# Where the identity matrix comes from: GpSimd's iota replaced by a VectorE construction in a normalised-attention kernel

## The chip, the cores and the metric

The kernel runs on one core of one Trainium2 chip. A core has five engines that work side by side and meet only at semaphores: TensorE (PE, matrix products, with its weight loads listed apart as PEld), VectorE (DVE), ScalarE (ACT, activation functions), GpSimd (POOL) and SyncE (SP, which here only starts DMAs). The metric is the device time of one execution in microseconds (us), as the median of several runs; less is better.

## What is computed

Inputs are q, k and v of shape (1, 32, 2048, 20) in bf16 and one temperature t per head.

```python
eps = 1e-6
qn = q / (jnp.sqrt((q * q).sum(axis=-1, keepdims=True)) + eps)
kn = k / (jnp.sqrt((k * k).sum(axis=-1, keepdims=True)) + eps)
logits = jnp.einsum('bhqd,bhkd->bhqk', qn, kn) * t[None, :, None, None]
attn = _softmax(logits, axis=-1)
return jnp.einsum('bhqk,bhkd->bhqd', attn, v)
```

## The kernel before

**Tiling.** The 32 heads are taken in 8 groups of 4, so that four heads of 20 numbers, padded to 32 each, fill 128 partitions. A group has 4 blocks of 512 queries and 16 tiles of 128 keys. One head, one block and one key tile make a unit: 2,048 units in all. For each unit TensorE multiplies a key tile with a query block (L794, "QK": 32 rows deep, 512 columns), the result is exponentiated, and TensorE multiplies it with the values (L816, "PV").

**Two ways to exponentiate.** In the first, ScalarE's exp (L995) takes a wave of two units, 1,024 columns, from one of two PSUM slots. There are 636 of these; 1,272 of the 2,048 units go this way. In the second, VectorE turns the logits into 16-bit integers that are the bits of an approximate power (L371), GpSimd makes two shifted copies by a 64-bit integer add (L384, INT64_ADD), and TensorE adds the copies up in PV. This second way starts only when 12% of a group has been handed out (`D_FROM`).

**Before any of this** q and k must be normalised and transposed. For the first group this is done in parts, so that work can begin early: `PARTS` cuts the 16 rows that each partition holds into rows 0 to 3 and rows 4 to 15. For the first part, `prep_ops` (L262) makes: squares (L305), their sums (L308), a square root on ScalarE (L323), the addition of eps (L324), a reciprocal (L337), the scaled k into the padded tile `kpad` (L350), the temperature (L361), and the scaled q into `qpad` (L350 again). All but the root are VectorE's, and the scaling of k is GpSimd's, because `scale` is called with `nr == 4` as its last argument (L356). TensorE then transposes the four rows of k and of q by a matrix product with the identity `idn` (L625), VectorE and ScalarE copy the results to `kT` and `qT` (L640, L637), and the first QK can start. The pads of `kpad` and `qpad` must have been cleared by then; GpSimd's memsets (L542) do that.

**The start.** GpSimd's first instruction is an iota (L551) that writes column minus row into a piece of the tile `accT`. Its next are the memsets that clear the pads and the tail of the values (L542) and fill `ind` (L554, L555), a tile of block indicators for the sums of later groups; two affine selects (L547) shape `ind` once the first k rows are scaled. VectorE's first are two memsets (L558, L560), the comparison of the iota's result with zero that gives `idn` (L562), and four memsets of a tile `nrc` (L567) that nothing reads. The squares stand behind these on VectorE's queue. TensorE starts with 18 products of zeros (L617), and between the real ones it does more such products of 128 columns (L613); both only keep it at work.

**Order.** `make_plan` (L478) simulates the five engines with costs in microseconds written into the program, picks at every step what each engine does next, and thereby fixes the instruction order of each engine; semaphore waits follow from the tiles read and written. In that simulation a VectorE operation with a lower priority number goes first among those that are ready. The first select is entered there with 8 us, the iota with 0.5 us. The hardware then executes each engine's list strictly in that order.

Of the kernel before, what the change touches and what calls it, by code (L numbers as in the profile page):

```python
# [8 lines left out]
F32 = mybir.dt.float32  # L9
# [85 lines left out]
NM_ROWS = 4  # L95
SQ_POOL = False
POOL_S = 3
REC_POOL = False
POOLPRIO = 3
PSLACK = 0.25  # L100
POOL_EXT = ("P1",)
# [70 lines left out]
def bass_standalone__qk_norm__prompt_kernel(  # L172
# [15 lines left out]
    with ExitStack() as es:  # L188
        sbuf = lambda name, shape, dt: es.enter_context(nc.sbuf_tensor(name, shape, dt))
# [12 lines left out]
        kpad = [sbuf(f"kpad{i}", [128, R, NH, 32], BF16) for i in range(2)]  # L202
# [6 lines left out]
        dI = sbuf("dI", [128, RING * QW], I16)  # L209
        dS = [dI] + [sbuf(f"dS{i}", [128, RING * QW], I16) for i in range(1, len(SHIFTS))]  # L210
        zt = sbuf("zt", [128, QW], BF16)
        nrc = sbuf("nrc", [128, 4], F32)
        idn = sbuf("idn", [128, 128], BF16)
        ind = sbuf("ind", [128, 5, 224], BF16)
        sqT = sbuf("sqT", [128, 2 * NH * R * D], BF16)
        nr0 = sbuf("nr0", [128, 2, NH, 4], F32)
        tmx = sbuf("tmx", [128, 1], F32)
        accT = sbuf("accT", [128, QG * 16, 32], F32)
        iot = accT[:, 0:4, :].rearrange("p b d -> p (b d)")
        rec = sbuf("rec", [128, QG * 16], F32)  # L220
        ost = [sbuf(f"ost{i}", [128, 4, R, D], BF16) for i in range(2)]

# [25 lines left out]
        def dve(name, n, rate, emit, reads, writes, ncols_fix=0.0, info=None):  # L248
            c = n * rate
            o = Op("DVE", name, emit, reads, writes, cost=0.069 + c + ncols_fix,  # L250
                   lat=0.135 + c + ncols_fix, info=info)

            o.port = name not in ("P1", "cp", "drain", "red", "inv", "rec")
            return o

        def pool_op(name, n, two, emit, reads, writes):
            c = POOL0 + n * (POOL2 if two else POOL1)
            return Op("POOL", name, emit, reads, writes, cost=c, lat=c + POOLL)

        R1, R2, R4 = 1 / 960.0, 1 / 1920.0, 1 / 3840.0  # L260

        def prep_ops(hg, r0, r1, a0=0, a1=2, pool=False):  # L262

            b = hg % 2
            nr, na = r1 - r0, a1 - a0
# [20 lines left out]
            for c0 in range(r0, r1, sqn * 2 // na) if not hg else ():  # L286
# [10 lines left out]
                if pool and SQ_POOL:  # L297
                    for c in range(0, nn, SQ_ROWS):
                        k0, k1 = c * D, min(c + SQ_ROWS, nn) * D
                        ops.append(pool_op("sq", na * NH * (k1 - k0), True,  # L300
                                           lambda e, o=s3[:, :, k0:k1], x=x3[:, :, k0:k1]: e.tensor_tensor(o, x, x, ALU.mult),
                                           kq, [("sqs", bs, c)]))
                else:
                    ops.append(dve("sq", w_, R2,
                                   lambda e, o=s3, x=x3: e.tensor_tensor(o, x, x, ALU.mult),  # L305
                                   kq, [("sqs", bs)] + [("sqs", bs, c) for c in range(R)]))
                ops.append(dve("red", w_, R1,
                               lambda e, o=o4, x=s4: e.tensor_reduce(o, x, AXIS_X, ALU.add),  # L308
# [12 lines left out]
            if nr == 4:  # L321
                n0 = nr0[:, :, :, :].rearrange("p a h r -> p (a h) r")
# [16 lines left out]
            def scale(a, pad, nm, whole):  # L339
                step = NM_ROWS if r0 else 16  # L340
                for c0, c1 in [(c, min(c + step, r1)) for c in range(r0, r1, step)]:
                    nn = c1 - c0

                    base = qk[b][:, a, :, c0:c0 + nn, :]
                    src = bass.AP(qk[b], base.offset, [base.ap[0], [R * D, NH], [D, nn], [1, D]])
                    rb_ = rn[b][:, a, :, c0:c0 + nn]
                    sc = bass.AP(rn[b], rb_.offset, [rb_.ap[0], [R, NH], [1, nn], [0, D]])
                    db = pad[b][:, c0:c0 + nn, :, 0:D]
                    dst = bass.AP(pad[b], db.offset, [db.ap[0], [32, NH], [NH * 32, nn], [1, D]])
                    emit = lambda e, o=dst, x=src, s=sc: e.tensor_tensor(o, x, s, ALU.mult)  # L350
                    rd, wr = [("qk", b, a, i) for i in parts] + [RN[a]] + [("qkx", b, i) for i in range(1, 4)] * (a == 0), [(nm, b, r) for r in range(c0, c0 + nn)]
                    ops.append(pool_op("nm" + nm[0], 4 * nn * D, True, emit, rd, wr) if whole else
                               dve("nm" + nm[0], 4 * nn * D, R1, emit, rd, wr))

            if a1 == 2:
                scale(1, kpad, "kpad", nr == 4)  # L356
            if a0 == 0:
                rq = rn[b][:, 0, :, r0:r1]
                tt = bass.AP(tb16, tb16[:, hg * NH:(hg + 1) * NH].offset,
# [28 lines left out]
        def part_op(hg, c):  # L388
            b = hg % 2
            f = lambda tl: tl[b][:, :, :, :].rearrange("p h r d -> p (h r d)")  # L390
            return dve("vh", NH * R * VW, R4, lambda e: e.tensor_single_scalar(f(vpart[c]), f(vaug), c, ALU.mult),
                       [("v", b, hh) for hh in range(NH)] + [("vz", b)], [("vh", b, c)])
# [28 lines left out]
        def load_qk(hg, a, part=None):  # L421
            b = hg % 2
            r0, r1 = (0, R) if part is None else PARTS[part]
            if a == 0 and hg == HG - 1:

                ops = []
                for x in range(4):
                    s_ = q[0, hg * NH:(hg + 1) * NH].rearrange("h (i x r) d -> x i h (r d)", x=4, r=R)[x]
                    d_ = qk[b][32 * x:32 * x + 32, a, :, :, :].rearrange("p h r d -> p h (r d)")
                    keys = [("qk", b, a, 0), ("qk", b, a, 1)]  # L430
                    ops.append(dma("ldq", lambda e, d=d_, s=s_: e.dma_start(d, s), keys if x else [], [("qkx", b, x)] if x else keys, 0.5, 4.0))
                return ops
            src = (q, k)[a][0, hg * NH:(hg + 1) * NH].rearrange("h (p r) d -> p h r d", p=128)[:, :, r0:r1, :]
            s_ = src.rearrange("p h r d -> p h (r d)")
            d_ = qk[b][:, a, :, r0:r1, :].rearrange("p h r d -> p h (r d)")
            return [dma("ld" + "qk"[a], lambda e: e.dma_start(d_, s_), [],
                        [("qk", b, a, i) for i in ((0, 1) if part is None else (part,))],
                        0.5, 4.0 if part != 0 else LOAD0)]
# [39 lines left out]
        def make_plan(share):  # L478

            P = Plan()  # L480
# [39 lines left out]
            def want_dve(op, prio):  # L520
                P.link(op)
                seq[0] += 1
                (pool_todo if op.eng == "POOL" else dve_todo).append([prio, seq[0], op])
# [5 lines left out]
            def finish(op, start, cost, lat):  # L529
                op.start, op.done = start, start + lat  # L530
                P.put(op)


            def pool_init(tm, ops):
                for o in ops:
                    P.link(o)
                    finish(o, tm, o.cost, o.lat)
                    tm += o.cost
                free_["POOL"] = tm

            def zeros(i, after=()):
                z = lambda ap_, val, key: Op("POOL", "z", lambda e: e.memset(ap_, val), after, [(key, i)], 0.5, 0.6)  # L542
                return [z(kpad[i][:, :, :, D:32], 0.0, "kz"), z(qpad[i][:, :, :, D:32], 0.0, "qz"),
                        z(vaug[i][:, :, :, D:D + 1], 1.0, "vz"), z(vaug[i][:, :, :, D + 1:VW], 0.0, "vz")]

            def select(tile, pattern, base, mult, op, key, cost):
# [1 line left out]
                          [key], [key], cost, cost + 0.1)  # L548

            band = ind[:, :, 96:128]  # L550
            pool_init(0.2, [Op("POOL", "iota", lambda e: e.iota(iot, [[-1, 128]], base=0, channel_multiplier=1,  # L551
                                                                allow_small_or_imprecise_dtypes=True),
                               [], [("accT", 0)], 0.5, 0.6)] + zeros(0) +
                           [Op("POOL", "z", lambda e: e.memset(ind[:, :, :], 0.0), [], ["ind"], 0.9, 1.0),  # L554
                            Op("POOL", "z", lambda e: e.memset(band, 1.0), ["ind"], ["ind"], 0.3, 0.4)])  # L555
            sels = [select(band, [[128, 5], [-D, 32]], 0, 1, ALU.is_ge, "ind", 8.0),
# [1 line left out]
            o = P.link(Op("DVE", "z", lambda e: e.memset(zt[:, :], 0.0), [], ["zt"], 0.25, 0.3))  # L558
            finish(o, 0.15, o.cost, o.lat)
            o = P.link(Op("DVE", "z", lambda e: e.memset(act_scr[:, :], 1.0), [], ["scr"], 0.1, 0.15))  # L560
            finish(o, 0.4, o.cost, o.lat)
            o = P.link(dve("idn", 128, R1, lambda e: e.tensor_single_scalar(idn[:, :], iot, 0.0, ALU.is_equal),  # L562
                           [("accT", 0)], ["idn"]))
            finish(o, 1.0, o.cost, o.lat)
            tm = 1.3
            for ap_, x, key in [(nrc[:, i:i + 1], x, "nrc") for i, x in enumerate((1e-30, 0.5, 1e-6, -1.0))]:
                o = P.link(Op("DVE", "z", lambda e, ap_=ap_, x=x: e.memset(ap_, x), [], [key], 0.08, 0.15))  # L567
                finish(o, tm, o.cost, o.lat)
                tm += o.cost

            free_["DVE"] = tm

            o = P.link(Op("ACT", "tab", lambda e: e.activation(act_scr[:, 0:16], act_scr[:, 0:16], ACT.Sqrt),
                          ["scr"], ["scr0"], 1.5, 1.6))
# [9 lines left out]
            o = P.link(load_qk(0, 0, 0)[0])  # L584
# [10 lines left out]
            for o in prep_ops(0, 0, 4, 0, 2):  # L595
                if o.name == "nrm":
                    o.eng = "ACT"
                    act_ops.append(P.link(o))
                    a = Op("ACT", "tab", lambda e: e.activation(act_scr[:, 16:32], act_scr[:, 16:32], ACT.Exp),
                           ["scr"], ["scr1"], 1.5, 1.6)  # L600
# [15 lines left out]
            o = Op("PE", "heat", None, ["zt"], [("psA", 0), ("psD", OB(0))])  # L616
# [35 lines left out]
            for r0, r1, a0, a1 in ((4, 16, 1, 2), (4, 16, 0, 1)):  # L652
# [16 lines left out]
                for w_ in ("q", "k")[a0:a1][::-1]:  # L669
                    for c0, c1 in ((8, r1) if w_ == "k" else (r0, r1),):  # L670
                        o = tr_op(0, w_, c0, c1)
                        o.reads.append((w_ + "z", 0))
                        want_sp(o)
            if share:
                for c in vpart:
                    o = part_op(0, c)
# [666 lines left out]
            while left:  # L1343
                progressed = False
                for e in P.order:
                    while pos[e] < len(P.order[e]):
                        o = P.order[e][pos[e]]
# [4 lines left out]
                        for d in sorted(o.deps, key=lambda d: -d.start):  # L1352
                            if d.eng == e and e in ("PE", "ACT") and d.sem is None:
                                continue
                            key, val = (d.sem.name if d.sem is not None else d.eng), (d.val if d.sem is not None else d.cnt)
# [128 lines left out]
```

## Time and profile before

| | before |
|---|---|
| median of 3 runs | 613.58 us (612.43 to 615.75) |
| profiled execution | 618.1 us, of which the profile's span is 616.4 us |
| mean granted TensorE clock | 0.974 of full speed |
| PE busy | 598.0 us |
| ACT busy | 589.2 us, 636 exps |
| DVE busy | 575.8 us |
| POOL busy | 500.0 us, 957 INT64_ADD |

How to read it: the profile is one execution, and its span runs from the first to the last instruction. A row of the timeline gives the start, the duration, engine, source line, operation, output and input, the number of merged instructions, and in square brackets how long the engine had been idle and what released it. "issue" stands for a wait on nothing that the profile shows. In the rows by stretch of time there stand, after the stretch and its length, the busy time and the count of records of PE, PEld, DVE, ACT and POOL, then the granted TensorE clock, the share of the DMA engines in use and their GB/s. The granted clock is shown from its changes; ahead of the first change it reads 1.00.

### The profile page before, as it was taken

To read this page: it belongs to the slowest core of one execution; us is meant where nothing else is said; L and a number is where in the kernel's file an instruction comes from. 1 tells how busy PE (TensorE), PEld (TensorE's weight loads), DVE (VectorE), ACT (ScalarE), POOL (GpSimd) and SP (SyncE) were. 2 spreads that over 40 slices of the span, in tenths; PEclk is the share of its full clock that TensorE was granted. 3 is DMA by queue.
4 is the path that set the end of the run, shared out by engine and by line. 5 is a ranking of instruction groups with operands and counts; after the bars stand their busy time and mean duration, and the time that the engine had idled before them with its cause. 6 is when DMAs were issued, how large, how long until landed. Compare 5 with 4: busy or idle time off the path is not lost.

```text
span 616.4 us, 16316 instructions
## 1 busy us (share of the span) xinstructions
PE 598.0 (97%) x6754; PEld 163.8 (27%) x6754; DVE 575.8 (93%) x949; ACT 589.2 (96%) x644; POOL 500.0 (81%) x975
## 2 busy tenths in 40 slices
PE   4999999999999999999999999999999999999995
PEld 1432222232222322232222322222222232222221
DVE  3759999999999999999999999999999999999994
ACT  2689999999999999999999999999999999999995
POOL 3148799787998969797898979978798887989994
PEclk8579999999999999999999989999999999999999
DMA  8330220611433060421306013060324303010000
GB/s 112 34 70 2 45 69 1 70 19 38 76 23 67 2 112 2 44 45 36 78 2 79 11 35 78 2 87 2 45 53 38 66 2 71 2 22 2 7 13 10
DMA packets 132144, 24.19 MB, mean 39 GB/s; under 512 B 121312, under 2 KB 132064, under 8 KB 132064
## 3 DMA queue, kind: packets, MB, share of 16 engines
q1 hardware_dynamic: 131264, 22.96, 24.2%
q8 instruction: 55, 0.90, 0.6%
q14 instruction: 25, 0.20, 0.1%
q10 hardware_dynamic: 800, 0.12, 0.1%
HBM read 7.87 MB, written 2.62 MB: 17 GB/s over the span
## 4 chain that ended last, share of the span: by engine, by line
ACT 79%; PE 18%; issue 1%; DVE 1%; POOL 0%; POOLq 0%; DVEq 0%
ACT pA L995 79%; PE psD L816 8%; PE psA L794 6%; PE psD L613 2%; PE psD L794 1%; DVE idn L562 0%; PE psD L625 0%; DVE ssum L308 0%; POOL kpad L350 0%; DVE accT L396 0%; PE psD L659 0%; DVE sqs L305 0%; DVE ost L410 0%; DVE qT L640 0%; DVE rn L337 0%
## 5 line engine op out<-in xcount | busy, mean ns | idle before, releaser
L995 ACT ACTIVATE pA<-psA 128x1024 f16<-128x1024 f32 (+1 forms) x636 | 584.9, 1227 | 8.4 <-PE psA L794 6.8
L384 POOL INT64_ADD dS<-dI x957 | 492.8, 531 | 87.4 <-DVE dI L371 23.3
L371 DVE TENSOR_SCALAR dI<-psD 128x512 int16<-128x512 f32 (+1 forms) x749 | 480.2, 698 | 17.7 <-PE psD L794 13.5
L794 PE MATMUL psA<-qT,kT 32*128 32x512 bf16 x1272 | 253.3, 391 | 4.1 <-ACT pA L995 2.5
L794 PE MATMUL psD<-qT,kT 32*128 32x512 bf16 x785 | 235.3, 385 | 0.0
L816 PE MATMUL psD<-dS,vaug 128*22 128x512 f16 x1552 | 191.7, 384 | 0.0
L816 PE MATMUL psD<-pA,vaug 128*22 128x512 f16 (+1 forms) x1272 | 173.4, 387 | 0.0
L816 PE MATMUL psD<-dI,vhalf 128*22 128x512 f16 x776 | 128.6, 385 | 0.0
L816 PE MATMUL psD<-dI,vaug 128*22 128x512 f16 x776 | 128.3, 384 | 0.0
L794 PEld LDWEIGHTS psA<-qT,kT 32*128 32x128 bf16 x1272 | 60.1, 91 | 252.1 <-ACT pA L995 244.4
L794 PEld LDWEIGHTS psD<-qT,kT 32*128 32x128 bf16 x785 | 56.1, 91 | 8.9 <-DVE dI L371 4.3
L816 PEld LDWEIGHTS psD<-dS,vaug 128*22 128x22 bf16 x1552 | 40.9, 89 | 53.5 <-issue 31.1
L816 PEld LDWEIGHTS psD<-pA,vaug 128*22 128x22 bf16 x1272 | 36.7, 89 | 51.7 <-issue 48.5
L816 PEld LDWEIGHTS psD<-dI,vhalf 128*22 128x22 bf16 x776 | 28.5, 89 | 26.8 <-issue 19.2
L816 PEld LDWEIGHTS psD<-dI,vaug 128*22 128x22 bf16 x776 | 28.5, 89 | 25.8 <-issue 19.7
L396 DVE STREAM_TRANSPOSE accT<-psD 128x512 f32<-128x512 f32 x32 | 22.5, 703 | 4.2 <-PE psD L816 4.2
L613 PE MATMUL psD<-zt 128*128 128x128 bf16 x151 | 18.9, 276 | 0.0
L613 PEld LDWEIGHTS psD<-zt 128*128 128x128 bf16 x151 | 12.7, 123 | 9.6 <-issue 9.6
L350 DVE TENSOR_TENSOR qpad<-qk,rn 128x1280 bf16<-128x1280 bf16 (+1 forms) x11 | 12.9, 1184 | 0.1
L410 DVE TENSOR_TENSOR ost<-accT,rec 128x1280 bf16<-128x1280 f32 (+1 forms) x11 | 12.8, 1160 | 0.1
L750 PE MATMUL psD<-ind,sqT 128*128 128x128 bf16 x140 | 12.0, 221 | 0.0
L278 DVE TENSOR_TENSOR sqs<-qk 128x1280 bf16<-128x1280 bf16 x14 | 11.9, 856 | 0.0
(54 smaller groups left out, 87.6 us busy)
## 6 DMA issues: line engine op xcount, KB each, us to landing
vaug<-in_v_dram SPq DMA_DIRECT2D x32, 80.0 KB, 4.4
qk<-in_k_dram SPq DMA_DIRECT2D x7, 320.0 KB, 4.3
out_dram<-ost SPq DMA_DIRECT2D x28, 80.0 KB, 1.9
qk<-in_q_dram SPq DMA_DIRECT2D x6, 320.0 KB, 4.1
qk<-in_q_dram SPq DMA_DIRECT2D x4, 80.0 KB, 3.0
out_dram<-ost SPq DMA_DIRECT2D x7, 40.0 KB, 2.0
qk<-in_k_dram SPq DMA_DIRECT2D x1, 240.0 KB, 3.6
qk<-in_q_dram SPq DMA_DIRECT2D x1, 240.0 KB, 4.2
```

Source lines behind the costliest of these rows:

```text
L278: ops.append(dve("sq", w_, R2, lambda e, o=sq, x=x3: e.tensor_tensor(o, x, x, ALU.mult), [("qk", b, a, i) for i in parts] + [("qkx", b, i) ...
L350: emit = lambda e, o=dst, x=src, s=sc: e.tensor_tensor(o, x, s, ALU.mult)
L371: lambda e: e.tensor_scalar(dst, psD[:, pb * QW:(pb + n) * QW], 1024.0 * LOG2E, 15360.0 - 1024.0 * LOG2K + SHIFTS[0], ALU.mult, ALU.add),
L384: lambda e: e.int64_add(o.bitcast(U64), x.bitcast(U64), add), rd, wr)
L396: return dve("drain", QW, R1, lambda e: e.transpose(accT[:, 16 * b:16 * b + 16, :].rearrange("p b d -> p (b d)"), psO_(sb)), [("psD", OB(s ...
L410: dve("omul", 320 * n, R1, lambda e: e.tensor_tensor(dst, num, rcb, ALU.mult), at + ar, [("ost", hg % 2, g) for g in range(g0, g1)]),
L613: return lambda e: e.matmul(bank, zt[:, 0:128], zt[:, 0:n], start=False, stop=False, skip_group_check=True)
L750: mms = [lambda e, g=g, j=j: e.matmul(dst, sqT[:, (5 * g + j) * 128:(5 * g + j + 1) * 128], ind[:, j, 96 - 32 * g:224 - 32 * g], start=g + ...
L794: return lambda e: e.matmul(dst, lhsT, rhs, tile_position=(32 * hh, 0))
L816: return lambda e: e.matmul(dst, lhsT, rhs, start=first, stop=last, skip_group_check=True, tile_position=(0, 32 * hh))
L995: a = Op("ACT", "exp", lambda e, s=src, d=dst: e.activation(d, s, ACT.Exp), [("psA", slot)], [("pA", pslot, i) for i in range(WAVES[slot]) ...
```

## The change

The iota goes, and so do the comparison that waited for it and the four unread memsets. VectorE builds the identity by itself: it clears `idn`, writes 0, 4, ..., 28 into every fourth column of a 32-column tile `num` (eight memsets), writes ones into the four diagonal 32x32 blocks of `idn` (four memsets), fills the columns between by adding 1, 2 and 3, transposes `num` in 32x32 blocks, compares it with its transpose, and multiplies the four column blocks of `idn` by the result. The clear, the memsets, the adds and the transpose enter the plan with priority 0, the compare and the multiply with 1.6, behind the first part's preparation at 1.5. GpSimd's list now begins with the memsets. The scaling of the first k rows moves from GpSimd to VectorE. The selects stay as they are, on GpSimd, behind the scaled k.

```diff
@@ tiles
-        nrc = sbuf("nrc", [128, 4], F32)
-        iot = accT[:, 0:4, :].rearrange("p b d -> p (b d)")
+        num, numT, numE = accT[:, 0, :], accT[:, 1, :], accT[:, 2, :]
@@ prep_ops
-                scale(1, kpad, "kpad", nr == 4)
+                scale(1, kpad, "kpad", False)
@@ make_plan
-            pool_init(0.2, [Op("POOL", "iota", lambda e: e.iota(iot, [[-1, 128]], base=0, channel_multiplier=1,
-                                                                allow_small_or_imprecise_dtypes=True),
-                               [], [("accT", 0)], 0.5, 0.6)] + zeros(0) +
+            pool_init(0.0, zeros(0) +
...
-            o = P.link(dve("idn", 128, R1, lambda e: e.tensor_single_scalar(idn[:, :], iot, 0.0, ALU.is_equal),
-                           [("accT", 0)], ["idn"]))
-            finish(o, 1.0, o.cost, o.lat)
-            tm = 1.3
-            for ap_, x, key in [(nrc[:, i:i + 1], x, "nrc") for i, x in enumerate((1e-30, 0.5, 1e-6, -1.0))]:
-                o = P.link(Op("DVE", "z", lambda e, ap_=ap_, x=x: e.memset(ap_, x), [], [key], 0.08, 0.15))
-                finish(o, tm, o.cost, o.lat)
-                tm += o.cost
-
+            tm = 0.6
             free_["DVE"] = tm
+            n4 = num.rearrange("p (a b) -> p a b", b=4)
+            zs = [(idn[:, :], 0.0, "idn")] + [(n4[:, a, 0:1], 4.0 * a, ("num", a)) for a in range(8)] + \
+                 [(idn[32 * a:32 * a + 32, 32 * a:32 * a + 32], 1.0, ("idb", a)) for a in range(4)]
+            for ap_, x, key in zs:
+                want_dve(Op("DVE", "z", lambda e, ap_=ap_, x=x: e.memset(ap_, x), ["idn"] * (key[0] == "idb"), [key], 0.07, 0.3), 0)
+            n0 = [("num", a) for a in range(8)]
+            for b in (1, 2, 3):
+                want_dve(Op("DVE", "z", lambda e, b=b: e.tensor_single_scalar(n4[:, :, b:b + 1], n4[:, :, 0:1], float(b), ALU.add),
+                            n0, [("num", -b)], 0.08, 0.4), 0)
+            nums = n0 + [("num", -b) for b in (1, 2, 3)]
+            want_dve(Op("DVE", "z", lambda e: e.transpose(numT, num), nums, ["numT"], 0.15, 0.4), 0)
+            want_dve(Op("DVE", "z", lambda e: e.tensor_tensor(numE, num, numT, ALU.is_equal), nums + ["numT"], ["numE"], 0.15, 0.4), 1.6)
+            i4, e4 = idn[:, :].rearrange("p (a b) -> p a b", b=32), bass.AP(accT, numE.offset, [numE.ap[0], [0, 4], [1, 32]])
+            want_dve(Op("DVE", "z", lambda e: e.tensor_tensor(i4, i4, e4, ALU.mult), ["idn", "numE"] + [("idb", a) for a in range(4)], ["idn", ("accT", 0)], 0.25, 0.4), 1.6)
```

More of the change, by code (lines that the diff above doesn't have):

```diff
@@ L97 @@
 POOL_S = 3
-REC_POOL = False
 POOLPRIO = 3
```

## The prediction

> **What bounds the kernel now.** I read the page first (span, clock by slices), then the chain of waits over the whole span.
>
> ```profile
> span 616.4 us, 16316 instructions
> PEclk8579999999999999999999989999999999999999
> ```
> ```profile
> 38.36 323.76 ACT pA L995 x353
> ```
>
> From 38.36 on ScalarE's exps follow each other without a gap, 353 in 323.76 us, 0.917 us each. An edit to the start cannot make that stage shorter; it can only let it begin earlier. So the question is what lies ahead of 38.36, and the clock row says that TensorE ran slow there. The timeline of the start:
>
> ```profile
> 0.31 0.10 POOL L1469 MEMSET const-float32-0.0<- 128x1 f32 x1 [0.31 <-issue]
> ...
> 0.92 0.27 DVE L558 MEMSET zt<- 128x256 uint32 x1 [0.92 <-PEq L1469]
> 1.15 0.09 DVE L560 MEMSET act_scr<- 128x32 f32 x1
> ...
> 1.65 5.20 PE L617 MATMUL psA<-zt 128*128 128x512 bf16 x17
> ...
> 8.09 0.24 POOL L551 IOTA accT<- 128x128 f32 x1 [7.60 <-issue]
> 8.29 0.73 POOL L542 MEMSET kpad<- 128x768 bf16 x1
> 8.36 1.74 DVE L562 TENSOR_SCALAR idn<-accT 128x128 bf16<-128x128 f32 x1 [7.13 <-POOL accT L551]
> ...
> 10.04 0.46 DVE L567 MEMSET nrc<- 128x1 f32 x4
> ...
> 10.16 1.23 POOL L554 MEMSET ind<- 128x1120 bf16 x1
> 10.49 0.49 DVE L305 TENSOR_TENSOR sqs<-qk 128x640 bf16<-128x640 bf16 x1
> ...
> 11.44 0.23 POOL L555 MEMSET ind<- 128x160 bf16 x1
> ...
> 12.13 0.18 DVE L324 TENSOR_SCALAR rsa<-nr 128x32 f32<-128x32 f32 x1 [0.20 <-ACT nr L323]
> 12.35 0.35 DVE L337 RECIPROCAL rn<-rsa 128x32 f32<-128x32 f32 x1
> 12.74 0.18 DVE L361 TENSOR_TENSOR rn<-rn,tb 128x16 f32<-128x16 f32 x1
> 12.79 0.73 POOL L350 TENSOR_TENSOR kpad<-qk,rn 128x320 bf16<-128x320 bf16 x1 [1.11 <-DVE rn L337]
> ...
> 12.95 0.91 DVE L350 TENSOR_TENSOR qpad<-qk,rn 128x320 bf16<-128x320 bf16 x1
> ...
> 13.57 0.61 PE L625 MATMUL psD<-idn,kpad 128*128 128x128 bf16 x4 [6.72 <-POOL kpad L350]
> ...
> 14.61 0.36 POOL L547 TENSOR_SCALAR_AFFINE_SELECT ind<-ind 128x160 bf16<-128x160 bf16 x1
> ...
> 15.17 0.62 PE L794 MATMUL psA<-qT,kT 32*128 32x512 bf16 x4 [0.57 <-DVE qT L640]
> ...
> 15.82 1.02 ACT L995 ACTIVATE pA<-psA 128x1024 bf16<-128x1024 f32 x1 [0.41 <-PE psA L794]
> ```
>
> GpSimd runs a memset at 0.31, but its iota only at 8.09, after 7.60 us of a wait that nothing in the profile explains. VectorE waits 7.13 us for the iota, holds 1.74 us in the compare, and reaches the squares at 10.49. From there to the first exp it is 15.82 - 10.49 = 5.33 us. TensorE is idle for 6.72 us, until 13.57. Did q and k arrive late too? The DMA view of the first 0.9 us says no:
>
> ```profile
> qk<-in_k_dram SPq DMA_DIRECT2D x1, 80.0 KB, 2.5
> qk<-in_q_dram ACTq DMA_DIRECT2D x1, 80.0 KB, 2.7
> ```
>
> Issued within that 0.9 us, both are there by 3.6 at the latest. The wait is the iota's alone.
>
> Now the clock, from the view by stretches of time, and the exps before 38.3, from the groups by line of 15.8 to 38.3:
>
> ```profile
> 11.00:12.00 1.00, 0.00 (x0) 0.00 (x0) 0.91 (x2) 0.13 (x1) 0.62 (x2) 0.62 0.87 157
> 20.00:30.00 10.00, 10.00 (x67) 4.51 (x63) 6.00 (x18) 6.87 (x7) 1.74 (x4) 0.50 0.21 32
> 38.00:39.00 1.00, 1.00 (x12) 0.29 (x8) 0.62 (x2) 0.66 (x1) 0.00 (x0) 0.73 0.00 0
> 40.00:42.00 2.00, 2.00 (x22) 0.51 (x19) 2.00 (x4) 2.00 (x3) 1.83 (x5) 1.00 0.00 0
> ```
> ```profile
> L995 ACT ACTIVATE pA<-psA 128x1024 f16<-128x1024 f32 (+1 forms) x15 | 15.2, 1024 | 6.9 <-PE psA L794 6.8
> ```
>
> A mean of 0.62 between 1.00 and 0.50 puts the fall at 11.24, 4.4 us into TensorE's idle time; 0.73 puts the return at 38.54. In between TensorE is busy all the time at half clock and ScalarE waits for it (6.8 of 6.9 us): 15 exps from 15.82 to 38.36 take 22.54 us. At 0.917 they would take 13.76. So the late start costs twice: its own delay, and 8.78 us because the idle time cooled the clock and the work of this stage did not warm it again for 27 us.
>
> **The change part by part.** *GpSimd's start.* The iota goes; the memsets start where the other engines do, at 0.92, and take 3.38 us (8.29 to 11.67 in the rows), to 4.30. The unexplained 7.2 us (0.92 to 8.09) may come back at the first select. That waits for the scaled k; its load would then run from about 7 to 14. Behind it on GpSimd stand the second select, the clears for the next group and the first INT64_ADD:
>
> ```profile
> 39.18 1.15 POOL L384 INT64_ADD dS<-dI  x3 [11.76 <-DVE dI L371]
> ```
>
> That comes 23.4 us after the first exp before and about 14.5 after it then, near 24: some 9 us of cover. I cost the select's wait at nothing; without that cover it is up to 7.2. [...]
>
> *VectorE's start.* Zeroes and ones end at 1.24. Then 13 memsets at 0.46/4 = 0.115: 2.74. Three adds: nearest row the 0.18 one of L324, 0.54: 3.28. Transpose and compare, 0.25 each with their waits (estimates from the same row): 3.78, then the squares. The multiply, some 0.3, fits into the wait for ScalarE's root. This is the low end, S = 3.8, just behind the arrival of q and k. The high end: L562 took 1.74 beside GpSimd's memsets, against 0.18 for L324 beside none. The adds are the same kind and run beside the memsets, which end at 4.30; if all three are held until then, S = 4.30 + 0.54 + 0.50, 5.3. [...] I take the middle, S = 4.6: 5.9 us earlier.
>
> *Scaled k on VectorE.* Uncrowded, one such op is 1.29/3 = 0.43:
>
> ```profile
> 19.24 1.29 DVE L350 TENSOR_TENSOR kpad<-qk,rn 128x320 bf16<-128x320 bf16 x3
> 39.18 0.68 PE L613 MATMUL psD<-zt 128*128 128x128 bf16 x9
> ```
>
> In series k, temperature and q take 0.43 + 0.18 + 0.43 and 0.15 of gaps: from 12.70 to 13.89 on the old axis, where q ended at 13.86 and k at 13.52 before. TensorE's q transposes wait for the same moment, k's start 0.3 earlier. Cost nothing; the bounds are -0.3 and +0.4.
>
> *The clock.* Warm products end at 6.85. The squares at 4.6 put k's transposes at 4.6 + 2.7, 7.3: TensorE idles 0.5 us, not 6.7, and stays warm unless the work behind it is too thin. How thin? [...]
>
> ```profile
> 360.00:361.00 1.00, 0.41 (x3) 0.10 (x2) 1.00 (x3) 1.00 (x3) 0.77 (x2) 1.00 0.00 0
> 361.00:362.00 1.00, 0.75 (x6) 0.25 (x6) 1.00 (x3) 1.00 (x3) 0.66 (x2) 1.00 0.76 151
> 362.00:363.00 1.00, 0.90 (x11) 0.20 (x10) 1.00 (x3) 1.00 (x3) 0.95 (x4) 0.91 1.14 217
> ```
>
> The clock fell at 362.8 after three us with 3, 6 and 11 products, 7 per us; at 40 to 42, with 11 per us, it stayed. The first stage has 67 products per 7 exps: at 0.917 per exp 10.4 per us, near the case that stayed. Around the first exp it is thinner: 8 transposes, the first 4 products and some 9 zero ones (0.68 us for 9) within three us make 21, or 7 per us, just where it fell. Hence a real chance of losing the clock; against it, 18 full products end only 0.5 us ahead. If it holds, 15 exps take 13.8 instead of 22.5, saving 8.7, and half-clock transposes and products ahead of the first exp shrink (0.61 and 0.62 each to about 0.4): 0.4. With the clock on, other things come late next: rows 4 to 15 of k, GpSimd's copies. I allow 1.5 us of new gaps (bounds 0 and 3, estimated from the 6.9 us that ScalarE idled). [...]
>
> **Sum.** 5.9 + 0.4 + 8.7 - 1.5 = 13.5 us. The profiled execution took 618.1, its span 616.4 with 1.7 around it; it would come to 604.6. The median of the runs is 613.58, 4.5 below the profiled one; taking the same microseconds off gives 600.1.
>
> **Rivals.** *The clock falls all the same.* The thin stretch around the first exp decides; only the earlier start is left, 613.6 - 5.9 = 607.7. *The wait isn't the iota's,* but that of GpSimd's first instruction here. For it: "issue" names no cause. Against: the memset at 0.31. Two clears of 0.73 would then end near 9.6 and hold q's transposes till there, which q's scaling released at 13.86 (12.95 + 0.91); the first exp comes 4.3 us earlier, the clock falls, 609.3. *VectorE's chain is longer than the wait it replaces.* If GpSimd's memsets hold adds, compare and multiply each for 1.74, as L562's row: 2.74 + 3 x 1.74 + 0.25 + 2 x 1.74 = 11.7, 1.2 us later than 10.49, and 614.8: slower. It decides from the fifth hold on (four end at 9.95). Against it: there are only 3.4 us of memsets to be held by.
>
> **How the numbers follow.** Forecast 0.68; clock falls 0.20; first instruction 0.06; long chain 0.04; 0.02 for the rest (the wait comes back at INT64_ADD too, 607). The forecast's own range: S from 3.8 to 5.3, gaps 0 to 3, and the whole order is planned anew, so a few exps may go to the other path or back at 0.917 each, say 2 us: 596 to 604. With the cold-clock case and its spread in S, 596 to 609. About 0.5%, 3 us, can be told from no change here. Faster by more than that, under 610.5: 0.92; same 0.05; slower 0.03.
>
> **What would show it.** GpSimd's first memset near 0.9; squares between 3.8 and 5.3; first exp near 9.5; the granted clock at 1.00 without a fall between the first warm-up and 40; the sixteenth exp near 24; an unexplained wait of about 7 us before the first select. A first exp behind 12, or a clock at 0.50 around 15, would make it wrong.

## The result, and the profile after

| | before | after |
|---|---|---|
| median (range, executions) | 613.0 us (612.22 to 615.75, 4) | 604.25 us (602.85 to 605.42, 4) |
| profiled execution, its span | 618.1 us, 616.4 us | 605.24 us, 603.5 us |
| mean granted TensorE clock | 0.974 | 0.990 |
| first exp | 15.82 | 8.46 |
| sixteenth exp | 38.36 | 22.97 |

The ratio of the times is 0.9848, with a 95% interval of 0.9807 to 0.989: 8.75 us less, against 13.5 us forecast. (In all comparisons below, executions more than 1.5% above the fastest of their kernel are left out of the ratios; the kernel before had some in each of them, the changed kernel none.)

The page of the changed kernel, with its span and its clock by slices, to be read against the two lines of the kernel before:

```profile
span 603.5 us, 16332 instructions
PEclk9999989999999999998999999999999999999999
```

The first three digits, 8, 5 and 7 before, are 9s: the low clock at the start is gone. Two 8s stand in the sixth and the nineteenth slice of 15 us (75 to 91 and 272 to 287). The chain of waits over the whole span shows what they do (start, length, what):

```profile
12.77 57.98 ACT pA L997 x63
...
79.70 196.27 ACT pA L997 x214
...
281.57 236.64 ACT pA L997 x258
```

Before, 353 exps ran in one piece. Now ScalarE is dense from 12.77, and the piece is broken twice, at 72 to 79 and at 277 to 281. The timeline of the start, whose rows answer one by one to those shown of before:

```profile
0.79 0.74 POOL L540 MEMSET kpad<- 128x768 bf16 x1 [0.29 <-POOLq L1471]
...
1.99 0.58 DVE L567 TENSOR_SCALAR accT<-accT 128x8 f32<-128x8 f32 x3
2.63 0.21 DVE L570 STREAM_TRANSPOSE accT<-accT 128x32 f32<-128x32 f32 x1
...
3.59 0.49 DVE L303 TENSOR_TENSOR sqs<-qk 128x640 bf16<-128x640 bf16 x1 [0.52 <-DMA qk<-in_q_dram]
3.95 0.23 POOL L551 MEMSET ind<- 128x160 bf16 x1
4.00 0.28 DVE L573 TENSOR_TENSOR idn<-idn,accT 128x128 bf16<-128x128 bf16 x1
...
5.91 0.49 DVE L348 TENSOR_TENSOR kpad<-qk,rn 128x320 bf16<-128x320 bf16 x1
...
6.52 0.49 DVE L348 TENSOR_TENSOR qpad<-qk,rn 128x320 bf16<-128x320 bf16 x1
...
6.66 0.39 PE L627 MATMUL psD<-idn,kpad 128*128 128x128 bf16 x4
...
8.46 3.77 ACT L997 ACTIVATE pA<-psA 128x1024 bf16<-128x1024 f32 x4 [0.19 <-PE psA L796]
...
11.74 0.40 PE L818 MATMUL psD<-pA,vaug 128*22 128x512 bf16 x4 [0.90 <-DMA vaug<-in_v_dram]
12.02 0.88 POOL L545 TENSOR_SCALAR_AFFINE_SELECT ind<-ind 128x160 bf16<-128x160 bf16 x2 [7.83 <-DVE rsa L334]
12.77 3.84 ACT L997 ACTIVATE pA<-psA 128x1024 f16<-128x1024 f32 x4 [0.54 <-PE psA L796]
```

GpSimd's memsets start at 0.79 and end at 4.18. The three adds beside them take 0.58 us together. The squares at 3.59 wait no longer for the identity but for q's DMA. TensorE's transposes follow the last warm-up product (which ended at 6.83), with no idle time. The first exp comes 7.36 us earlier than before. GpSimd then stands idle for 7.83 us ahead of the selects, and nobody waits for it. One gap is new: TensorE waits 0.90 us for the values, and the fifth exp 0.54 us behind it.

What fills GpSimd's 7.83 us? The releaser named, VectorE's L334, has nothing to do with `ind`. The view of single lines shows more than the timeline (count, durations in ns, first and last start in us), for the select and for the INT64_ADD:

```profile
L545 POOLq MODIFY_POOL_CONFIG  x2: 11/11/11, 4.2 to 4.2; - x2
```
```profile
L382 POOL INT64_ADD dS<-dI x957: 387/402/1046, 24.6 to 594.2; - x192
L382 POOLq MODIFY_POOL_CONFIG  x2: 11/11/11, 18.8 to 18.9; - x2
```

Ahead of the first operation of each of these two kinds, GpSimd's sequencer has two instructions MODIFY_POOL_CONFIG of 11 ns, and the operation starts 7.8 and 5.8 us after them. So the wait has a mark in the trace, and it starts when the queue gets there (4.2, as the last memset ends), not when the operands are ready. I go on calling it a load, as in the prediction; the trace shows its mark and its length, not what is done in it. The kernel before has the same pair at 0.9, ahead of its iota, and the second at 28.2, ahead of its INT64_ADD.

Last the clock, by stretches of 1 us (busy time and count of PE, PEld, DVE, ACT, POOL, then the granted clock):

```profile
10.00:11.00 1.00, 0.81 (x9) 0.34 (x7) 0.86 (x5) 1.00 (x2) 0.00 (x0) 1.00 1.20 71
11.00:12.00 1.00, 0.26 (x4) 0.10 (x4) 0.90 (x4) 1.00 (x2) 0.00 (x0) 1.00 0.84 115
...
70.00:71.00 1.00, 0.94 (x6) 0.18 (x3) 1.00 (x3) 1.00 (x2) 0.85 (x3) 1.00 0.00 0
71.00:72.00 1.00, 0.96 (x8) 0.28 (x6) 1.00 (x2) 1.00 (x2) 1.00 (x2) 1.00 0.00 0
72.00:73.00 1.00, 1.00 (x11) 0.21 (x10) 0.69 (x2) 1.00 (x2) 1.00 (x3) 0.81 0.06 16
73.00:74.00 1.00, 1.00 (x8) 0.13 (x4) 0.22 (x1) 0.75 (x2) 1.00 (x3) 0.50 0.00 0
```

At 10 to 12 TensorE did 9 and 4 products, about as few as in two of the three us ahead of the fall in the kernel before (3 and 6), and the clock stayed at 1.00. It fell at 72.6 instead (0.81 puts it there) and came back at 79.4; ScalarE lost 2.1 us. The second fall, from 277.4 to 280.8, cost it 0.8 us.

In the balance of the two profiles the first exp is 7.4 earlier, and the fifteen exps behind it take 14.5 us instead of 22.5, 8.0 less. That is 15.4 at the sixteenth exp (12.77 + 11 x 0.927 = 22.97), and 12.9 at the end of the span: some 2.5 us were given back, 2.9 of falls in place of the single one of 0.8 before, and the rest in the last part. Yet the medians are only 8.75 apart. The experiments are about this difference first.

### The profile page after: what moved, and what is told of

Its sections match the earlier page's. It is cut to its first block, busy times and chain, and to the rows that moved or that the text cites. A ratio compares the mean times of both kernels' runs of the same rounds, so it can differ in the third digit from the quotient of the medians.

```text
span 603.5 us, 16332 instructions
## 1 busy us (share of the span) xinstructions
PE 590.9 (98%) x6754; PEld 159.5 (26%) x6754; DVE 575.9 (95%) x964; ACT 588.5 (98%) x644; POOL 500.1 (83%) x973
## 4 chain that ended last, share of the span: by engine, by line
ACT 81%; PE 16%; SPq 1%; DMA 1%; DVE 0%; issue 0%
ACT pA L997 81%; PE psD L818 9%; PE psA L796 6%; PE psD L796 1%; SPq L444 1%; DMA vaug<-in_v_dram 1%; SPq L434 0%; PE psD L615 0%; DVE accT L394 0%; DVE ost L408 0%; SPq L582 0%; DVE rec L407 0%
## 5 line engine op out<-in xcount | busy, mean ns | idle before, releaser
L369 DVE TENSOR_SCALAR dI<-psD 128x512 int16<-128x512 f32 (+1 forms) x749 | 480.1, 697 | 14.5 <-PE psD L796 10.7
L796 PE MATMUL psA<-qT,kT 32*128 32x512 bf16 x1272 | 250.6, 387 | 4.2 <-ACT pA L997 2.5
L818 PEld LDWEIGHTS psD<-dI,vhalf 128*22 128x22 bf16 x776 | 28.4, 89 | 27.3 <-issue 20.0
L394 DVE STREAM_TRANSPOSE accT<-psD 128x512 f32<-128x512 f32 x32 | 22.5, 703 | 4.2 <-PE psD L818 4.2
L615 PE MATMUL psD<-zt 128*128 128x128 bf16 x151 | 14.1, 221 | 0.0
L348 DVE TENSOR_TENSOR kpad<-qk,rn 128x1280 bf16<-128x1280 bf16 (+1 forms) x11 | 12.6, 1155 | 0.1
```

What stands on the lines that cost most here:

```text
L369: lambda e: e.tensor_scalar(dst, psD[:, pb * QW:(pb + n) * QW], 1024.0 * LOG2E, 15360.0 - 1024.0 * LOG2K + SHIFTS[0], ALU.mult, ALU.add),
L394: return dve("drain", QW, R1, lambda e: e.transpose(accT[:, 16 * b:16 * b + 16, :].rearrange("p b d -> p (b d)"), psO_(sb)), [("psD", OB(s ...
L615: return lambda e: e.matmul(bank, zt[:, 0:128], zt[:, 0:n], start=False, stop=False, skip_group_check=True)
L796: return lambda e: e.matmul(dst, lhsT, rhs, tile_position=(32 * hh, 0))
L818: return lambda e: e.matmul(dst, lhsT, rhs, start=first, stop=last, skip_group_check=True, tile_position=(0, 32 * hh))
```

## The experiments

**Theory:** the gain is the earlier start and a clock that no longer falls, in about the shares that the two profiles show. **Rival A:** the load on GpSimd was never the matter; the clock alone, or VectorE's work alone, makes the time. **Rival B:** the profiled execution of before was an odd one; in most, the low clock costs little, and the earlier start is nearly all of the gain.

**The kernel before once more, unchanged.**

> The kernel before, once more, unchanged. Theory (half of the gain is clock): its stage from the first exp to the sixteenth again lies at a granted clock of 0.50 and takes 20 to 23 us, and executions with a higher mean clock are shorter; 612 to 616 us. Rival (the profiled 618.1 was one odd execution and the low clock belonged to it): the stage takes about 14 us at clock 1.00 and the time is still 612 to 613.

Median 619.5 us (611.36 to 632.39, 10), ratio to the other executions of before 0.9992 (0.9933 to 1.005). This profiled execution took 611.36 us. ScalarE's timeline in it, and the clock:

```profile
16.16 1.94 ACT L995 ACTIVATE pA<-psA 128x1024 bf16<-128x1024 f32 x2 [0.41 <-PE psA L794]
18.85 1.02 ACT L995 ACTIVATE pA<-psA 128x1024 f16<-128x1024 f32 x1 [0.75 <-PE psA L794]
20.25 25.85 ACT L995 ACTIVATE pA<-psA 128x1024 f16<-128x1024 f32 x28 [0.38 <-PE psA L794]
```
```profile
9.00:10.00 1.00, 0.00 (x0) 0.00 (x0) 1.00 (x1) 0.00 (x0) 1.00 (x3) 0.97 0.98 58
...
20.00:21.00 1.00, 1.00 (x11) 0.36 (x9) 0.88 (x3) 0.75 (x1) 0.00 (x0) 0.91 0.09 5
```

The clock falls here too (0.97: at 9.94), but is back at 20.18, after 10.2 us instead of 27.3. Fifteen exps take 15.2 us (16.16 to 20.25 + 12 x 0.923), 1.4 more than the dense 13.8, not 8.8 more. So the stage recurs and its length doesn't: Rival B. The granted clocks of the other executions say which of the two profiles is the usual one. Of the fifteen in the ratio, twelve stand at 0.983 to 0.985 and took 612.1 to 613.7 us, near the second profile (0.987); two stand at 0.976 and 0.973 and took 617 and 618, like the first (0.974).

**The changed kernel with 4 warm-up products in place of 18.** The output stays whole.

```diff
-for i in range(HEAT0 - 1)]
+for i in range(3)]
```

> The changed kernel with 4 instead of 18 products of zeros at the start, every other instruction in the same order; it leaves out no part of the result. TensorE then has worked only 1.7 us and idles from about 3 to 6.7. Theory (the clock is worth as much as the earlier start): the squares still start near 3.6 and the first exp near 9, but the fifteen exps behind it take about 22 us at clock 0.50 instead of 14.4, and the time is 611 to 613. Rival A (the gain is the earlier start, the clock is incidental): 604 to 605. [...]

Median 610.51 us (605.36 to 614.44, 10 executions), ratio to before 0.9937 (0.9886 to 0.9988). Four executions took 605.4 to 606.5 and four 614.3 to 614.4, with 610.2 and 610.8 between. ScalarE's timeline in one of 614.3, with the rows between left out, and TensorE's first group in the groups by line of 12 to 42:

```profile
8.87 1.94 ACT L997 ACTIVATE pA<-psA 128x1024 bf16<-128x1024 f32 x2 [0.41 <-PE psA L796]
11.56 1.02 ACT L997 ACTIVATE pA<-psA 128x1024 f16<-128x1024 f32 x1 [0.75 <-PE psA L796]
...
42.00 8.36 ACT L997 ACTIVATE pA<-psA 128x1024 f16<-128x1024 f32 x9 [0.29 <-PE psA L796]
```
```profile
L796 PE MATMUL psA<-qT,kT 32*128 32x512 bf16 x42 | 12.7, 596 | 0.0
```

The clock row can't be used here, as it reads 1.00 ahead of its first change. The products show it: a mean of 596 ns, as in the slow stage of before (0.62 us), against 387 over the changed kernel, all the way to 42. Here the clock did not fall; after four products it had not risen yet (in the changed kernel, with 18, the warm-up products start 0.43 us apart until 4.2 and 0.22 apart from 4.5 on). The first exp is about as early as in the changed kernel, and the time is 9 us above its profiled 605.24. The clock is thus worth up to some 9 us when it stays low for 33 us behind the first exp. The four executions at 605.4 to 606.5 are 1 or 2 us above the changed kernel's median; that they had the clock back early isn't shown, as there is no trace of them. Neither theory alone has this: the early start needs the warm-up to be worth anything for certain.

**The kernel before with 48 warm-up products in place of 18,** so that TensorE isn't idle during the iota's wait.

```diff
-for i in range(HEAT0 - 1)]
+for i in range(47)]
```

> The kernel before with 48 instead of 18 products of zeros at the start, every other instruction in the same order, so that TensorE works until the identity is there (about 13.2). Theory: first exp still near 15.8 (up to 1 us later), clock 1.00 from then on, fifteen exps in 14 to 15 us instead of 22.5, 604.5 to 607 us. Rival A (clock incidental): 612 to 614. Rival B (clock comes back by itself after some 3.4 to 7 us): 610 to 611.

Median 610.65 us (608.52 to 611.64, 5), ratio 0.9954 (0.9929 to 0.9979). ScalarE's timeline is dense from the first exp:

```profile
15.10 35.85 ACT L995 ACTIVATE pA<-psA 128x1024 bf16<-128x1024 f32 x39 [0.19 <-PE psA L794]
```

That is all that the theory asks of the clock, and by the ratio it brings 2.8 us against before, not 8; 0.7 of it is the earlier first exp (15.10 against 15.82). Rival B's 610 to 611 is right and the theory's share of the clock is wrong: in the second profile of before the clock came back at 20.18, 6.3 us after TensorE's work had set in again at 13.9, within Rival B's 3.4 to 7 (the two falls of the changed kernel, 3.4 and 6.8 us long, span the same range). (A fall at 352 to 363 cost this execution 2.8 us, so part of the gain was given back, as in the changed kernel; but the two executions with the highest clock, 0.997, took 608.52 and 609.11, above the theory's 604.5 to 607 as well.)

**The changed kernel with the iota put back at the head of GpSimd's list,** writing a piece of `accT` that nobody reads.

```diff
-pool_init(0.0, zeros(0) +
+pool_init(0.0, [Op("POOL", "iota", lambda e: e.iota(iot, ...), [], [("accT", 1)], 0.01, 0.02)] + zeros(0) +
```

> The changed kernel with the iota back at the head of GpSimd's list, its result read by nobody; VectorE still builds the identity. Theory (the 7 us wait belongs to the iota and holds what stands behind it on GpSimd): first clear at 8.3, pads clear at 9.6, so q's transposes wait and the first exp comes near 11, 2.5 us later than in the changed kernel; 606 to 607.5 if the clock holds, 611 to 614 if TensorE's idle time of 2 us cools it. Rival (the wait is that of VectorE on the iota and nothing else needs it gone): first exp near 8.5 and 604 to 605.

Median 609.03 us (603.99 to 610.33, 6), ratio 0.9951 (0.9922 to 0.998). VectorE's three adds and GpSimd's timeline:

```profile
1.99 0.32 DVE L570 TENSOR_SCALAR accT<-accT 128x8 f32<-128x8 f32 x3
...
8.24 0.24 POOL L550 IOTA accT<- 128x128 f32 x1 [7.74 <-issue]
8.43 0.73 POOL L541 MEMSET kpad<- 128x768 bf16 x1
...
11.97 0.77 POOL L546 TENSOR_SCALAR_AFFINE_SELECT ind<-ind 128x160 bf16<-128x160 bf16 x2
...
26.71 3.44 POOL L383 INT64_ADD dS<-dI  x8 [6.69 <-DVE dI L370]
```

The load is back ahead of the iota, the selects have none, and INT64_ADD keeps its own. The pads are cleared 7.6 us later, and the first exp stands at 11.36. So an iota whose result nobody reads costs 5 us by the medians (609.03 against 603.79 of the changed kernel in the experiment below; 7 us by the two ratios to before), by what is queued behind it on GpSimd. Rival A falls. The adds took 0.32 us here, with GpSimd in its wait, and 0.58 beside the memsets in the changed kernel: the memsets slow them, by 0.26 us in all. (The profiled execution is the fastest of the six, 603.99, with the clock at 1.00 until the last exps were done; the others had a mean of 0.985 to 0.99 and took 4 to 6 us more.)

**The changed kernel once more.**

> The changed kernel once more, unchanged, for the ratio beside the others. Theory (the start is worth 7 us, the clock between 1.4 us where the old low stage lasts 10 us and 9 us where it lasts 27): 602.8 to 605.5, 8 to 10 us below the kernel before. Rival (the 12.9 us between the two profiled spans is the usual gain): 600 to 601.

Median 603.79 us (602.77 to 607.74, 6), ratio 0.9834 (0.9795 to 0.9872). The result stands. The profiled execution, 606.13, lost the clock at 275.2 to 278.6 and at 346.9 to 357.1, and kept it at 72. The falls keep to a few places of the program (before lost it at 363 to 366 in one profile, at 283 to 286 in the other); which of them is hit differs from one execution to the next.

The first exp comes at 8.84 here, 0.38 later than in the first profile of the changed kernel. The warm-up products run until 7.40, longer than q's scaling (6.97), and the transposes wait behind them. So the start has met its next limit: in four of the six profiles with this start the warm-up products end between 7.40 and 8.26 and the first exp comes at 8.84 to 9.70; in the other two they end at 6.83 and 7.01 and it comes at 8.46 and 8.45. No run tried a number between 4 and 18.

**The changed kernel with the scaling of k back on GpSimd.**

```diff
-scale(1, kpad, "kpad", False)
+scale(1, kpad, "kpad", nr == 4)
```

> The changed kernel with the first k rows scaled by GpSimd again, all else the same. Theory (this move cost and gave nothing: in series on VectorE or beside it on GpSimd, q is ready at the same moment): first exp at 8.4 to 9.0, 603 to 606, no difference to the changed kernel that can be told. Rival (without the iota in front, GpSimd's scaling would carry a wait of its own of 6 to 7 us): first exp at 12 to 15 and 608 to 612.

Median 611.7 us (606.77 to 623.04, 12), ratio 0.9955 (0.9921 to 0.999). From the timeline:

```profile
11.13 0.72 POOL L348 TENSOR_TENSOR kpad<-qk,rn 128x320 bf16<-128x320 bf16 x1 [6.91 <-issue]
...
11.91 0.61 PE L627 MATMUL psD<-idn,kpad 128*128 128x128 bf16 x4 [5.29 <-POOL kpad L348]
...
12.50 0.35 POOL L545 TENSOR_SCALAR_AFFINE_SELECT ind<-ind 128x160 bf16<-128x160 bf16 x1
```

I took this part for one that costs nothing either way, and was wrong. The load now stands ahead of k's scaling, on the path to the first product. TensorE idles 5.29 us, the clock falls (to 0.50 from 10.8 to 17.6), and the first exp is at 14.15. The selects, on the other hand, have no wait. So one load serves the iota, this TENSOR_TENSOR and the select, and whichever is first on GpSimd pays it (idle times of 7.74, 6.91 and 7.83 us in the three orders). With either of the two edits undone, the ratio to before is 0.995 or 0.996 and not 0.983: about three quarters of the gain hang on both together.

**The changed kernel with the values loaded ahead of q's rows 4 to 15.**

```diff
-for a in (1, 0):
-    want_sp(load_qk(0, a, 1)[0])
+want_sp(load_qk(0, 1, 1)[0])
 for o in load_v(0):
     want_sp(o)
+want_sp(load_qk(0, 0, 1)[0])
```

> The changed kernel with the first group's four loads of v issued ahead of the load of q's rows 4 to 15, all other orders the same. Theory (the new gap of 0.54 us between the fourth and the fifth exp is a wait for v): first PV at 11.0 or before, no gap of the exps behind the first, sixteenth exp 0.5 us earlier; 602.5 to 605, too little to be told by the time. Rival (q's rows now land late): the squares of q's second part start behind 15.2 and the gap only moves.

Median 604.27 us (602.02 to 607.18, 6), ratio 0.9842 (0.9805 to 0.988). ScalarE's and TensorE's rows:

```profile
1.65 6.18 PE L619 MATMUL psA<-zt 128*128 128x512 bf16 x17
...
7.67 0.39 PE L627 MATMUL psD<-idn,kpad 128*128 128x128 bf16 x4
...
9.27 11.11 ACT L997 ACTIVATE pA<-psA 128x1024 bf16<-128x1024 f32 x12 [0.19 <-PE psA L796]
...
11.58 0.40 PE L818 MATMUL psD<-pA,vaug 128*22 128x512 bf16 x4
```

The gap behind the fourth exp is gone, but this run alone doesn't show why. The first exp is 0.8 later, because the warm-up products ran until 7.83, and a later first exp closes the gap by itself: it is absent in the second profile of the changed kernel too, with the values in their old place and the first exp at 8.84. The first product with the values, at 11.58, also missed the forecast of 11.0. The last experiment separates the two causes. In time nothing can be told: the gap was 0.5 us, and the executions lie 5 us apart.

**The changed kernel with `TWICE` at 2:** a parameter of the kernel by which the plan lets TensorE do a QK group twice, at the points where it would otherwise be thinly used.

```diff
-TWICE = 1
+TWICE = 2
```

> The changed kernel with TWICE = 2: the first way's QK products are issued twice where a block ends and TensorE is thinly used; the plan around those places changes with it. Theory (the falls of the clock in mid-kernel come from thin stretches at block ends and cost about 1 us for each window of 3.4 us): no fall between 40 and 580 us, ScalarE's waits there under 0.5 us, 601.5 to 603.5. Rival (the doubled products delay the next wave more than the clock gives): the clock holds but 605 to 608.

Median 601.58 us (601.22 to 601.94, 6), ratio 0.9791 (0.9762 to 0.9819). From its page:

```profile
span 599.9 us, 16301 instructions
...
L997 ACT ACTIVATE pA<-psA 128x1024 f16<-128x1024 f32 (+1 forms) x636 | 583.4, 1226 | 0.2 <-PE psA L796 0.2
```

Between 20 and 580 ScalarE doesn't idle at all (2.9 us in the changed kernel, 2.1 in its fall of 6.8 us and 0.8 in that of 3.4) and the clock stays at 1.00. The executions lie 0.7 us apart instead of 5, and none overlaps with those of the changed kernel in the same run (602.77 to 607.74). What does it isn't settled: the trace has only 2 more products of the first way's QK (1,274 against 1,272), but the plan behind the first doubled group differs, as 946 INT64_ADD in place of 957 show, with the same 636 exps. The doubling wasn't tried apart from this new plan.

**The same again, and with the values' loads ahead.**

> The changed kernel with TWICE = 2 once more, for the comparison with the next one. Theory: 601 to 602 again, no fall of the clock in mid-kernel. Rival (the first result was a lucky stretch of phases): single executions at 604 to 606 with a mean clock under 0.99.

> TWICE = 2 and the four loads of v ahead of q's rows 4 to 15. Theory (the wait for v costs a gap of about 0.5 us and nothing else): 600.5 to 601.5, at most 0.6 us below the version without it, and no gap of the exps between the first and the sixteenth. Rival (q's rows land later, or the wait for v was hidden in most executions): the same time within 0.3 us, or longer.

601.7 us (601.08 to 602.14, 6), ratio 0.9788 (0.9741 to 0.9835), and 601.37 us (600.93 to 601.74, 6), ratio 0.9785 (0.9739 to 0.9832). The gain of `TWICE` is there again, on another chip. ScalarE's and TensorE's rows with the earlier values:

```profile
8.45 9.27 ACT L997 ACTIVATE pA<-psA 128x1024 bf16<-128x1024 f32 x10 [0.19 <-PE psA L796]
...
10.76 0.40 PE L818 MATMUL psD<-pA,vaug 128*22 128x512 bf16 x4
```

The first exp is as early as in the first profile of the changed kernel, the values are met at 10.76 and not at 11.74, and there is no gap: the wait for the transfer was its cause. In time the 0.33 us are no shown gain, as the two ranges overlap. All twelve executions of the two versions lie below all ten of the changed kernel (602.77 to 607.74), which was measured in other comparisons.

## Why the prediction was right, and where it was not

**The number.** The measured 604.25 lies 4.15 us above the 600.1 that was forecast and 0.25 outside the forecast's own range of 596 to 604; it lies inside the wider range, 596 to 609, which was drawn for a clock that falls. The clock at the start did not fall. So the time came out within the wider range for another reason than that range was drawn for, and this much is luck.

**The bound.** Right: behind the start the exps go on at 0.92 to 0.93 us each, and what the edit brings is brought by the sixteenth exp.

**GpSimd's start and the select.** The memsets at 0.79 (0.9 forecast) and a hidden wait of 7.8 us (7 forecast) were right. The place was wrong: I let the load begin when k is scaled, from 7 to 14; it began at 4.2, behind the last memset, and ended at 12.0. The wait at INT64_ADD, to which I gave 0.02, came as well: 5.8 us from 18.8. The first VectorE integers were ready at about 23.6 and the add ran at 24.62, so 1.0 us showed on GpSimd, and none on ScalarE. The kernel before had this load too, inside the 11.76 us in which it waited for VectorE. Where INT64_ADD's data was ready earlier, its load takes 5.5 to 5.8 us in the traces; the first load takes 6.9 to 7.8.

**VectorE's start.** Forecast 4.6, bounds 3.8 and 5.3; measured 3.59, below both bounds. VectorE's chain up to the compare ends at 3.07, and the squares then wait for q. Two terms were too big. The 13 memsets, put at 1.50 us, took 0.80 (1.19 to 1.99). The hold by GpSimd's memsets, taken at some 0.8 in the middle of the bounds, did not come: the three adds took 0.58 us beside the memsets and 0.32 beside none, a slowing of 0.26. The end of the old chain to the first exp, 4.93 by the forecast (5.33 - 0.4), was 4.87.

**k on VectorE.** Its cost was right: k's scaling starts at 5.91 and q's ends at 7.01, 1.10 us for the two and the temperature, as in the forecast (0.43 + 0.18 + 0.43, with gaps). What I missed is what it avoids: undone, it takes 611.7 - 603.79 = 7.9 us of the gain back.

**The clock, where the forecast failed.** "Taking the same microseconds off gives 600.1": the 8.7 us were read in an execution that took 4.5 us more than the median, and the excess lay in that very stage. The shift to the median took off what the median didn't have. With the second profile of before the sum is 16.16 - 8.46 = 7.7 for the start, and 15.2 - 14.5 = 0.7 for the fifteen exps, 8.4 in all against 8.75 measured. The gap of 0.5 is inside this. (With the second profile of the changed kernel it is 7.3 and 1.3, as its first exp comes later and no gap follows.) So the clock's term, 8.7, is about 1.2 in the usual execution (0.7 and the gap), 7.5 us less; the start (1.0 us more than forecast) and the gaps (1.0 less) made up for about a quarter of that by chance. The half of the argument that foretold the changed kernel held: warm from the zero products on, no fall until 40. The stretch around the first exp was less thin than counted: 5, 16 and 16 products in the three us from 7 to 10, 37 and not 21, as more zero products ran in it. To count products of all shapes alike was an estimate; no run shows that they weigh the same for the clock. Nor do the runs show one amount of work that brings a low clock back: in the second profile of before it took 6.3 us, in the first 25.0 (13.57 to 38.54), and in one execution with fewer warm-up products it stayed low for 33 us behind the first exp, while TensorE was busy but did few products per us (66 in the ten from 20 to 30).

**New gaps.** 1.5 us allowed, 0.54 found, and at the values' transfer, not at k's later rows or GpSimd's copies. What the forecast did not name is the wait for the warm-up products, 0.4 to 1.2 us of the first exp in four of six profiles.

**The order planned anew.** I allowed 2 us for exps that change the path. There were none: 636 exps and 957 INT64_ADD as before, and TensorE's, ScalarE's and SyncE's lists are the same, VectorE's and GpSimd's differ in the edited start alone. What I did not allow for are the later falls of the clock, 2.9 us in this profile against 0.8.

**The rivals.** The clock didn't fall at the start. GpSimd's first memset at 0.79 rules out the wait of a first instruction. VectorE's long chain would have needed holds of 1.74 us each; the adds lost 0.26 us together.

## What to carry to other kernels

Before you cost a stage from a profile, see how far that execution stands from the median, and where: an excess that lies in the stage that your edit removes must not be taken off the median as well. The unexplained wait ahead of GpSimd's first operation of a kind belonged to the kind, not to the operation (6.9 to 7.8 us for whichever of iota, TENSOR_TENSOR and select came first): ask which operation becomes the first of it, and what stands behind that. If such a wait can't go, put it where its engine has nothing else to do, and ahead of nothing that others wait for. And when a start gets shorter, look at what was sized for the old one: here the warm-up products became the next wait.

## What the runs showed of the hardware

The load on GpSimd is visible in the view of a single line, as two MODIFY_POOL_CONFIG of 11 ns, where the timeline says "issue" or names a bystander. It comes once for iota, TENSOR_TENSOR and the select together (6.9 to 7.8 us) and once for INT64_ADD (5.5 to 5.8, where its data was ready earlier); memsets run without it (from 0.79 in the changed kernel).

The clock's low stretches last 3.4 us (277.4 to 280.8), 6.8 (72.6 to 79.4), 10.2 and 27.3: one, two, three and eight times 3.41; the full stretch between the two falls of the changed kernel, 79.4 to 277.4, is 58 times as long. Why the same program meets more low stretches in one execution than in another is not shown. The times go with the granted clocks: the changed kernel's five executions at 0.994 to 0.996 took 602.77 to 603.26 us, the four at 0.985 to 0.990 605.24 to 607.74.

How thin the work may be can be counted. Go on in steps of 3.41 us from each trace's changes of the clock, and count the products that start in each step (long and short ones alike; a few records may be missing). From 12 us on, the twelve traces hold 2,052 steps. In the step that follows, the clock is low behind each of the 17 steps with 22 products or fewer and full behind each of the 2,004 with 27 or more; behind the 31 in between it is the one or the other. The us from 11 to 12 with its 4 products shares its step with full ones, 31 products in all; the step that ends with the fall at 72.6 holds 26. In the slow stage of before a busy TensorE starts only 20 to 25 products per step (67 in the ten us from 20 to 30), at the edge of this band. That would explain why a low clock, once there, can last 3 steps or 8; it is argued and not tested.
